# A growing lead for the scores at the start of a two-problem attention kernel, with TensorE transposes of the remainder's P in the ramp and round the change of weights

## The chip, the core and the metric

The kernel runs on one core of a Trainium2 chip. Times are device microseconds (us). The kernel before was run three times: 1224.69, 1225.98 and 1227.50 us, median 1225.98 us. One execution was taken by the hardware profiler; its own time is 1227.16 us.

Engines are called as in the profile: PE is TensorE's matmul, PEld its weight load, DVE VectorE, ACT ScalarE, POOL GpSimd, and SP the engine whose queue issues all DMAs here.

## What is computed

Two independent attention blocks A and B of the same shape, bfloat16, whose outputs stand side by side:

```python
B, Sq, D = 16, 144, 448;  H, Sk, Dh = 16, 512, 256
q = (x @ wq).reshape(B, Sq, H, Dh).transpose(0, 2, 1, 3)
scores = einsum("bhqd,bhkd->bhqk", q, k_cache) * Dh ** -0.5
p = softmax(scores)                                  # over the 512 keys
o = einsum("bhqk,bhkd->bhqd", p, v_cache)
out = o.transpose(0, 2, 1, 3).reshape(B, Sq, H * Dh) @ wo
# result: concatenate([out_A, out_B], axis=-1)
```

## The kernel before, in words

**Units and groups.** A unit U is one head of one batch element; there are 2 x 256 = 512 of them (0 to 255 are A, 256 to 511 B). The 144 queries of a unit are split: 112 rows ("a") have a score matmul of their own, and the remaining 32 rows ("b", the remainder) of four units are packed together to 128 rows, a quad G. Eight units (two quads) form a group SG; there are 64 groups. A group's K (2 MB) comes by one DMA that transposes it, and V comes by quads (1 MB each).

**What one unit does**, with the names and lines of the profile:

- Q: eight matmuls into the PSUM bank `qp_ps` (L322), copied to `qt_sb` by DVE (L334) or ACT (L338).
- SA: the scores of the 112 rows, two matmuls into one of two banks `sa_ps` (L424). Then max on DVE (L435), exp with its row sum on ACT (L446), the reciprocal on DVE (L456), and on POOL the multiplication of P by it (L464).
- SB, once a group: the remainder's scores of eight units, 16 matmuls into the two banks `sb_ps` (L348), with max, exp (L371), reciprocal (L381) and multiplication (L389) for each quad.
- TA: P of the 112 rows is transposed by four PE instructions into a bank of `sa_ps` (L477), copied to `pt_sb` by DVE (L487).
- The remainder's P is transposed for a whole group by one DMA from `pb_sb` to the single buffer `pbt_sb` (L399), and POOL copies it, a quad at a time, to its place in `pt_sb` (L410, `t_copy_ptb`).
- PV: eight matmuls of V and P into `ot_ps` (L510), copied by ACT into `ring` (L525).
- OP: the output projection over finished rows of 128 (L548), two matmuls at a time, at 2.5 matmuls a slot from slot 34 on; the result is copied and stored.

**Order.** A planner written in Python walks over slots i. Each engine's instructions run in the order in which this walk emits them; a scheduler adds the semaphore waits that the buffers need. Slot i has PV of unit i, TA of unit i+2, SA of unit i+14, Q of unit i+22, and SB of a group when its first SA is due. So the walk starts with 22 slots with Q and without PV; slot 0 is the first with PV. "Lead of the scores" is the distance between SA and PV: 14 units.

**DMAs** are in a list of (slot, order), walked by the same loop, so SP issues them in one fixed order and a waiting one holds those behind it: x0, weights wq 0 and 1, K0, wq 2 and 3, K1, the remainder's P of group 0, V0 to V2, x1, K2, and so on. There are two buffers for K, five for V, two for x. K of group n+2 may be issued once the last SA of group n has run. From the second group on, each pair of groups n, n+1 (n even) has the transposes of P at slots 8n-4 and 8n+2, K at 8n-3 and 8n+2, four V at 8n+5 to 8n+8, and x every 32 units. wo is loaded by eight parts for each problem, at slots 21 and 37 (and 256 later for B). The wq of B replaces that of A by four parts, at slots 229, 229, 232 and 235, behind three V of slot 229:

```python
plan((5, 5, 8, 11)[hg] + NU - 32, lo, dl, t_load_wq, 1, hg)
```

Q(256), the first that needs them, stands in slot 234.

Of the kernel before, what the change touches and what calls it, by code (L numbers as in the profile page):

```python
# [5 lines left out]
BF16 = mybir.dt.bfloat16  # L6
# [116 lines left out]
def bass_concat_heads__mha_block_cached__gqa_block_cached__near_ridge_kernel(  # L123
# [19 lines left out]
    Bn, SQ, D = A_x.shape  # L143
# [4 lines left out]
    NU = Bn * H  # L148
    NT = NP * NU
    NG = NT // 4  # L150
    HG = H // 4
    NCH = (Bn * SQ + 127) // 128
    RP = NCH * 128
# [4 lines left out]
    NWG = NWO // WOG  # L158
    NPC = NWO // OPP

    LQ, LS, LT = 22, 14, 2
    LSB = 14
    NK, NV, NXG = 2, 5, 2
    WO_AT = ((21, 37), (21, 37))
    OP_FROM = (34, 34)
    XB = 2
    assert Bn % XB == 0
    NQT, NPA, NPB, NPT, NST, NSTB, NOST = 12, 14, 2, 8, 4, 2, 3
    NPBT = 1
# [1 line left out]
    RC = RS * 128  # L171
    OP_DELAY = 2
    assert NT % 8 == 0
    NSG = NT // 8
    NXGT = NP * Bn // XB

    of = out.rearrange("b q e -> (b q) e")

    with contextlib.ExitStack() as es:
# [23 lines left out]
        ot_ps = [ps("ot_ps%d" % i, [128, 512], F32) for i in range(2)]  # L203
        op_ps = ps("op_ps", [128, 512], F32)
        pta_ps = [t.bitcast(BF16) for t in sa_ps]

        S = _Sched()
        sem_names = list(COMPUTE)
# [25 lines left out]
        def t_ident():  # L234
            ones = pa_sb[:, 0, 0:128]

            def e1(g):
                return g.memset(ones, 1.0)
            S.add(POOL, e1, writes=[(("pa", 0), "ones")], name="ones")

            def e2(g):
                return g.affine_select(ident[:], ones, pattern=[[1, 128]], compare_op=ALU.is_equal,
                                       fill=0.0, base=0, channel_multiplier=-1)
            S.add(POOL, e2, reads=[(("pa", 0), "ones")], writes=[("ident", 0)], name="ident")

        def t_wqzero():
            def e(v):
# [53 lines left out]
        def t_load_v(G):  # L301
# [5 lines left out]
                return q.dma_start(v_sb[:, sl, :, :], src).then_inc(sems["v%d" % sl], 16)  # L307
            S.add(SP, e, writes=[(("v", sl), G)], dma_sem="v%d" % sl, name="v%d" % G)

        def t_q(U):  # L310
            pr, b, h = unit(U)
            XG = (pr * Bn + b) // XB
            xsl = XG % NXG
            xo = (b % XB) * SQ
            hg = h // 4

            def e(t):
                ins = None
                for kc in range(4):
                    for dc in range(2):  # L320
                        c0 = h * DH + dc * 128
                        ins = t.matmul(qp_ps[:, dc * SQ:(dc + 1) * SQ], lhsT=wq_sb[:, kc, c0:c0 + 128],  # L322
                                       rhs=xt_sb[:, xsl, kc, xo:xo + SQ], start=(kc == 0 and dc == 0),
                                       stop=(kc == 3), skip_group_check=True)
                return ins
            S.add(PE, e, reads=[(("wq", hg), pr), ("wqz", 0), (("xt", xsl), XG)], writes=[("qp", ("q", U))],
                  banks=["qp"], name="Q%d" % U)

        def t_evac_q(U):
            sl = U % NQT  # L330
            src = qp_ps[:, 0:2 * SQ].rearrange("p (c q) -> p c q", c=2)
            if (U - LQ + LSB) % 8 in (1, 3, 5, 6):
                def e(v):
                    return v.tensor_scalar(qt_sb[:, sl, :, :], src, 1.0 / 16.0, None, op0=ALU.mult)  # L334
                S.add(DVE, e, reads=[("qp", ("q", U))], writes=[(("qt", sl), U)], banks=["qp"], name="eq%d" % U)
            else:
                def e(a):
                    return a.activation(qt_sb[:, sl, :, :], src, AF.Copy, scale=1.0 / 16.0)  # L338
                S.add(ACT, e, reads=[("qp", ("q", U))], writes=[(("qt", sl), U)], banks=["qp"], name="eq%d" % U)

        def t_sb(SG):
            def e(t):
# [51 lines left out]
        def t_ptb_dma(SG):  # L394
            psl = SG % NPB
            tsl = SG % NPBT

            def e(q):
                return q.dma_start_transpose(pbt_sb[:, tsl, :, :, :].rearrange("p g c q -> p (g c) q"),  # L399
                                             pb_sb[:, psl, :, :].rearrange("p g k -> p (g k)")).then_inc(  # L400
                    sems["pb%d" % tsl], 16)
            S.add(SP, e, reads=[(("pb", psl, g), (2 * SG + g, 1)) for g in range(2)], writes=[(("pbt", tsl), SG)],
                  dma_sem="pb%d" % tsl, name="pb%d" % SG)

        def t_copy_ptb(G):
            tsl = (G // 2) % NPBT
            s0 = (4 * G) % NPT

            def e(g):
                return g.tensor_copy(pt_sb[:, s0:s0 + 4, :, QA:SQ],  # L410
                                     pbt_sb[:, tsl, G % 2, :, :].rearrange("p c (j q) -> p j c q", j=4))
            S.add(POOL, e, reads=[(("pbt", tsl), G // 2)], writes=[(("ptb", s0 + j), 4 * G + j) for j in range(4)],
                  name="cptb%d" % G)

        def t_sa(U):
# [52 lines left out]

        def t_ta(U):
            psl = U % NPA  # L470
            bank = (U + LS - LT + 1) % 2

            def e(t):
                src = pa_sb[0:QA, psl, :].rearrange("q (p c) -> q c p", c=4)
                ins = None
                for c in range(4):
                    ins = t.transpose(pta_ps[bank][:, c * 128:c * 128 + QA], src[:, c, :], ident[0:QA, 0:QA])  # L477
                return ins
            S.add(PE, e, reads=[(("pa", psl), (U, 1)), ("ident", 0)], writes=[(("sap", bank), ("t", U))],
                  banks=["sa%d" % bank], name="TA%d" % U)  # L480

        def t_evac_pta(U):
            sl = U % NPT
            bank = (U + LS - LT + 1) % 2

            def e(v):
                return v.tensor_copy(pt_sb[:, sl, :, 0:QA],  # L487
# [94 lines left out]
        t_act_warm()  # L582
        t_wqzero()
        t_ident()
        s_min = -LQ - 24
        dma_plan = []

        def plan(at, lo, dl, fn, *args):
            assert lo <= at < dl, (fn.__name__, args, lo, at, dl)
            dma_plan.append((at, len(dma_plan), fn, args))  # L590

        def plan_k(at, SG):
            plan(at, 8 * (SG - NK) + 7 - LS + 1 if SG >= NK else s_min, 8 * SG - LSB, t_load_k, SG)

        def plan_v(at, G):
            plan(at, 4 * (G - NV) + 3 + 1 if G >= NV else s_min, 4 * G, t_load_v, G)

        def plan_pb(at, SG):
            plan(at, 8 * SG - LSB + 5, 8 * SG - 1, t_ptb_dma, SG)

        plan(s_min, s_min, -LQ, t_load_x, 0)
        for hg in range(HG):
            plan(s_min + (1 if hg < 2 else 3), s_min, 4 * hg - LQ, t_load_wq, 0, hg)
        plan_k(s_min + 2, 0)
        plan_k(s_min + 4, 1)
        for G in range(3):
            plan_v(-7, G)
        for pr in range(NP):
            for wg in range(NWG):
                plan(pr * NU + WO_AT[pr][wg // 4], s_min, pr * NU + OP_FROM[pr] + wg, t_load_wo, pr, wg)  # L610
        for n in range(0, NSG, 2):
            t = 8 * n
            XG = (t + 32) // (XB * H)
            if (t + 32) % (XB * H) == 0 and XG < NXGT:
                plan(t - 4, (XG - 1) * XB * H - LQ, XG * XB * H - LQ, t_load_x, XG)
            plan_pb(t - 4 if n else -8, n)
            if n + 2 < NSG:
                plan_k(t - 3, n + 2)
            plan_pb(t + 2, n + 1)
# [3 lines left out]
                if 2 * n + 3 + j < NG:  # L623
                    plan_v(t + at, 2 * n + 3 + j)
        for hg in range(HG):
            dl = NU + 4 * hg - LQ
            lo = NU - H + 4 * hg + 3 - LQ + 1
            plan((5, 5, 8, 11)[hg] + NU - 32, lo, dl, t_load_wq, 1, hg)
        dma_plan.sort(key=lambda t: t[:2])

        u_tail0 = NT - H
# [32 lines left out]
        while True:  # L664
            while dma_plan and dma_plan[0][0] <= i:
                _sl, _sq, fn, args = dma_plan.pop(0)
                fn(*args)
            sgi, ph = divmod(i + LSB, 8)
            do_sb = ph == 0 and 0 <= sgi < NSG
            ga, gb = 2 * sgi, 2 * sgi + 1  # L670
            ok = 0 <= sgi < NSG
            if ok and ph == 1:
                t_exp_b(ga)
            if ok and ph == 3:
                t_exp_b(gb)
            if ok and ph == 2:
                t_recip_b(ga)
                t_norm_b(ga)
            if ok and ph == 4:
                t_recip_b(gb)  # L680
                t_norm_b(gb)
            while stores and stores[0][1] <= i and (i % 16 in (9, 10, 11) or i >= NT - 4):
                t_store(stores.pop(0)[0])
            if do_sb and sgi == 0:
                t_sb(sgi)
            u = i + LQ
            if 0 <= u < NT:
                t_q(u)
                t_evac_q(u)
            if do_sb and sgi > 0:  # L690
                t_sb(sgi)
            u = i + LS
            if 0 <= u < NT:
                t_sa(u)
                t_max(u)
                t_exp(u)
            if i % 8 == 7 and 0 <= i + 1 < NT:
                t_copy_ptb((i + 1) // 4)
            if i % 8 == 1 and 0 <= i < NT:
                t_copy_ptb((i + 3) // 4)  # L700
            u = i + LS - 1
            if 0 <= u < NT:
                t_recip(u)
                t_norm(u)
            u = i + LT
            if 0 <= u < NT:
                t_ta(u)
                t_evac_pta(u)
            if ok and ph == 0:
                t_max_b(ga)  # L710
            if ok and ph == 2:
                t_max_b(gb)
            u = i
            if 0 <= u < NT:
# [92 lines left out]
```

## Time and profile before

| | us |
|---|---|
| median of three runs | 1225.98 |
| the profiled execution | 1227.16 |
| its span in the profile | 1225.4 |
| PE busy | 1167.7 (95%) |
| PEld busy | 877.0 (72%) |
| ACT busy | 745.6 (61%) |
| DVE busy | 730.3 (60%) |
| POOL busy | 728.6 (59%) |

The DMA engines move 310.87 MB at a mean of 254 GB/s. A digit in the page's rows of forty slices is the busy share of 30.6 us in tenths; PEclk is TensorE's granted clock in tenths of full speed. Matmuls are pipelined, so the start of one to the start of the next says more than the duration of one. In a row of the timeline the bracket is the engine's idle time just before it and what ended it.

### The profile page before, as it was taken

Reading aid. Unit: us, or ns where it says so; the run is one execution under the profiler, and the core shown is the slowest. Engines: PE = TensorE matmul, PEld = TensorE weight load, DVE = VectorE, ACT = ScalarE, POOL = GpSimd, SP = SyncE. Lnnn points to the kernel's source line nnn. Section 1 sums busy time; section 2 is a strip of 40 time slices with the busy share of each in tenths; the row PEclk is TensorE's granted clock in tenths of the full one; section 3 lists DMA queues with packets and bytes.
Section 4 is the critical chain, followed back from the end, with each engine's and each line's share of the span. In section 5 each row is a group of like instructions: output and inputs, shape, how many; then the busy total and the mean of one; then the engine's idle time right before and its main releaser. Section 6 shows DMA issues by size and latency. Waiting matters only on the chain.

```text
span 1225.4 us, 32870 instructions
## 1 busy us (share of the span) xinstructions
PE 1167.7 (95%) x13440; PEld 877.0 (72%) x13440; DVE 730.3 (60%) x2051; ACT 745.6 (61%) x2213; POOL 728.6 (59%) x774
## 2 busy tenths in 40 slices
PE   5698899999999999999899989999999999999999
PEld 3476667777777777777567757777777777777766
DVE  2577456666666566666456646666666666666661
ACT  2476466666666566666556656666666666666662
POOL 0676556666666666666456646656666665666661
PEclk9899899999999999999899989999999999999999
DMA  9999999999999999999999999999999999999982
GB/s 219 266 271 280 286 275 216 259 263 271 269 229 237 268 277 257 272 242 257 289 282 256 227 290 283 273 266 265 218 262 265 264 256 277 255 225 260 257 209 55
DMA packets 698583, 310.87 MB, mean 254 GB/s; under 512 B 616512, under 2 KB 629312, under 8 KB 698432
## 3 DMA queue, kind: packets, MB, share of 16 engines
q1 hardware_dynamic: 698432, 308.77, 106.3%
q8 instruction: 105, 1.72, 0.6%
q14 instruction: 46, 0.38, 0.1%
HBM read 148.90 MB, written 4.13 MB: 125 GB/s over the span
## 4 chain that ended last, share of the span: by engine, by line
PE 78%; DMA 15%; DVE 3%; POOL 2%; issue 2%; SPq 0%; ACT 0%; DVEq 0%
PE qp_ps L322 17%; PE ot_ps L510 17%; PE sa_ps L424 16%; PE op_ps L548 16%; DMA kt_sb<-in_A_k_cache_dram 8%; PE sa_ps L477 7%; PE sb_ps L348 6%; DMA kt_sb<-in_B_k_cache_dram 5%; POOL pa_sb L464 1%; DVE stat L435 1%; DMA v_sb<-in_A_v_cache_dram 1%; DVE qt_sb L334 1%; PE qp_ps L548 0%; DVE pt_sb L487 0%; DMA pbt_sb<-pb_sb 0%
## 5 line engine op out<-in xcount | busy, mean ns | idle before, releaser
L464 POOL TENSOR_TENSOR pa_sb<-pa_sb,stat 112x512 bf16<-112x512 bf16 x512 | 532.8, 1041 | 458.7 <-DVE stat L456 430.5
L446 ACT ACTIVATE pa_sb<-sa_ps,stat 112x512 bf16<-112x512 f32 x512 | 351.9, 687 | 408.1 <-DVE stat L435 405.7
L435 DVE TENSOR_REDUCE stat<-sa_ps 112x1 f32<-112x512 f32 x512 | 354.0, 691 | 366.2 <-PE sa_ps L424 361.7
L322 PE MATMUL qp_ps<-xt_sb,wq_sb 128*128 128x144 bf16 x4096 | 346.5, 229 | 22.2 <-DMA wq_sb<-in_A_wq_dram 9.4
L322 PEld LDWEIGHTS qp_ps<-xt_sb,wq_sb 128*128 128x128 bf16 x4096 | 290.7, 99 | 100.9 <-issue 15.5
L510 PE MATMUL ot_ps<-pt_sb,v_sb 128*128 128x144 bf16 x4096 | 343.1, 227 | 9.0 <-POOL pt_sb L410 8.3
L424 PE MATMUL sa_ps<-kt_sb,qt_sb 128*112 128x512 bf16 x1024 | 315.8, 390 | 4.7 <-DVE pt_sb L487 3.5
L510 PEld LDWEIGHTS ot_ps<-pt_sb,v_sb 128*128 128x128 bf16 x4096 | 270.2, 98 | 9.7 <-POOL pt_sb L410 8.6
L548 PE MATMUL op_ps<-wo_sb,ring 128*128 128x448 bf16 x1120 | 275.5, 353 | 0.0
L477 PEld LDWEIGHTS sa_ps<-ident,pa_sb 112*128 112x128 bf16 x2048 | 159.9, 114 | 109.2 <-ACT pa_sb L446 32.2
L525 ACT ACTIVATE ring<-ot_ps 128x288 bf16<-128x288 f32 (+8 forms) x512 | 189.9, 371 | 27.1 <-PE ot_ps L510 27.0
L487 DVE COPY pt_sb<-sa_ps 128x448 bf16<-128x448 bf16 x512 | 191.1, 373 | 17.7 <-PE sa_ps L477 17.7
L477 PE MATMUL sa_ps<-ident,pa_sb 112*128 112x112 bf16 x2048 | 187.6, 214 | 0.4 <-ACT pa_sb L446 0.4
L334 DVE TENSOR_SCALAR qt_sb<-qp_ps 128x288 bf16<-128x288 f32 x256 | 117.0, 457 | 103.1 <-PE qp_ps L322 102.6
L389 POOL TENSOR_TENSOR pb_sb<-pb_sb,stat 128x512 bf16<-128x512 bf16 x128 | 133.3, 1041 | 0.0
L424 PEld LDWEIGHTS sa_ps<-kt_sb,qt_sb 128*112 128x112 bf16 x1024 | 96.9, 130 | 47.3 <-issue 28.8
L338 ACT ACTIVATE qt_sb<-qp_ps 128x288 bf16<-128x288 f32 x256 | 105.9, 414 | 40.3 <-PE qp_ps L322 40.0
L548 PEld LDWEIGHTS op_ps<-wo_sb,ring 128*128 128x128 bf16 x1120 | 96.2, 98 | 32.0 <-issue 0.4
L446 ACT ACTIVATION_READ_ACCUMULATOR pa_sb<-sa_ps,stat 112x1 f32 x512 | 98.9, 193 | 0.0
L410 POOL COPY pt_sb<-pbt_sb 128x512 bf16<-128x512 bf16 x128 | 78.2, 611 | 21.3 <-PE ot_ps L510 10.9
L348 PE MATMUL sb_ps<-kt_sb,qt_sb 128*32 128x512 bf16 x1024 | 72.1, 405 | 18.6 <-DMA kt_sb<-in_A_k_cache_dram 12.3
L371 ACT ACTIVATE pb_sb<-sb_ps,stat 128x512 bf16<-128x512 f32 x128 | 88.3, 690 | 0.0
(20 smaller groups left out, 306.3 us busy)
## 6 DMA issues: line engine op xcount, KB each, us to landing
v_sb<-in_A_v_cache_dram SPq DMA_DIRECT2D x64, 1024.0 KB, 9.4
v_sb<-in_B_v_cache_dram SPq DMA_DIRECT2D x64, 1024.0 KB, 9.4
out_dram<-ost_sb SPq DMA_DIRECT2D x36, 112.0 KB, 10.2
wo_sb<-in_A_wo_dram SPq DMA_DIRECT2D x8, 448.0 KB, 5.0
wo_sb<-in_B_wo_dram SPq DMA_DIRECT2D x8, 448.0 KB, 5.7
wq_sb<-in_A_wq_dram SPq DMA_DIRECT2D x4, 768.0 KB, 6.6
wq_sb<-in_B_wq_dram SPq DMA_DIRECT2D x4, 768.0 KB, 13.1
pbt_sb<-pb_sb SPq DMA_TRANSPOSE x64, 4.6
```

Of the source, the lines that this page charges most:

```text
L322: ins = t.matmul(qp_ps[:, dc * SQ:(dc + 1) * SQ], lhsT=wq_sb[:, kc, c0:c0 + 128], rhs=xt_sb[:, xsl, kc, xo:xo + SQ], start=(kc == 0 and dc ...
L348: ins = t.matmul(sb_ps[jj // 4][32 * j:32 * j + 32, :], lhsT=qt_sb[:, U % NQT, dc, QA:SQ], rhs=kt_sb[:, dc, (U % (8 * NK)) * SK:(U % (8 * ...
L389: return g.tensor_tensor(pb_sb[:, psl, G % 2, :], pb_sb[:, psl, G % 2, :], stat[:, RINVB + sl:RINVB + sl + 1].to_broadcast([128, SK]), op= ...
L424: ins = t.matmul(sa_ps[bank][0:QA, :], lhsT=qt_sb[:, U % NQT, dc, 0:QA], rhs=kt_sb[:, dc, ko:ko + SK], start=(dc == 0), stop=(dc == 1))
L435: return v.tensor_reduce(stat[0:QA, NEG + sl:NEG + sl + 1], sa_ps[bank][0:QA, :], axis=AX.X, op=ALU.max, negate=True)
L446: return a.activation(pa_sb[0:QA, psl, :], sa_ps[bank][0:QA, :], AF.Exp, bias=stat[0:QA, NEG + sl:NEG + sl + 1], scale=1.0, accum_out=stat ...
L464: return g.tensor_tensor(pa_sb[0:QA, psl, :], pa_sb[0:QA, psl, :], stat[0:QA, RINV + sl:RINV + sl + 1].to_broadcast([QA, SK]), op=ALU.mult)
L477: ins = t.transpose(pta_ps[bank][:, c * 128:c * 128 + QA], src[:, c, :], ident[0:QA, 0:QA])
L487: return v.tensor_copy(pt_sb[:, sl, :, 0:QA], pta_ps[bank][:, 0:512].rearrange("p (c q) -> p c q", c=4)[:, :, 0:QA])
L510: ins = t.matmul(ot_ps[ob][:, dc * SQ:(dc + 1) * SQ], lhsT=v_sb[:, vsl, j, c * DH + dc * 128:c * DH + (dc + 1) * 128], rhs=pt_sb[:, sl, c, ...
L525: ins = a.activation(ring[:, 2 * h:2 * h + 2, c0:c0 + n1], src[:, :, 0:n1], AF.Copy)
L548: ins = t.matmul(acc[0:m, 0:D], lhsT=ring[:, c, col0:col0 + m], rhs=wo_sb[:, c, :], start=(c == first), stop=(c == last))
```

## The change

The lead is no longer fixed. `LAGS` gives the distance between the start of group n's scores (SB, then its SA) and its first PV: 7 for group 0, then 5, 6, 7 and so on to 14 for group 10 and all later ones. So groups 1 to 10 start at slots 3, 10, 17, 24, 31, 38, 45, 52, 59 and 66, seven slots apart, and the first slot of each of groups 1 to 9 has two SA. From slot 82 on the order is that of before. Q runs eight units ahead of SA, as before; the first eight Q come together one slot before the first SA, over four PSUM banks (`q_bank`), with 12 matmuls on zeros before them and 16 behind them (`t_warm`).

For groups 0 to 7 and 28 to 37 (`TB_SG`) the remainder's P is transposed by PE (`t_tb`, four instructions a quad, into a bank of `sb_ps`) and copied by DVE (`t_evac_tb`), and its DMA is left out. In the ramp the two TB stand three and five slots behind SB, but not before slot 8n-7; for groups 28 to 37 both stand in slot 8n-7, one slot before the next group's SB. Bank choice of TA (`ta_bank`): the bank that the slot's last SA doesn't use.

The DMA order of the ramp is written anew: x0, wq 0 and 1, K0, wq 2 and 3, V0, K1, V1, V2, K2, V3, V4, x1, K3, and so on, K and then two V a group. wo of A comes by pairs at slots 12, 18, 26 and 33. wq 0 and 1 of B stand at 228.9, ahead of the V of slot 229.

```diff
-    LQ, LS, LT = 22, 14, 2
-    LSB = 14
+    LT = 2
+    LAGS = (7, 5, 6, 7, 8, 9, 10, 11, 12, 13, 14)
+    RAMP = 8
+    TB_SG = set(range(RAMP)) | set(range(NSG // 2 - 4, NSG // 2 + 6))
-    WO_AT = ((21, 37), (21, 37))
+    WO_AT = ((12, 18, 26, 33), (277, 277, 293, 293))
+    N_WARM = (12, 16)
...
+        ptb_ps = [t.bitcast(BF16) for t in sb_ps]
...
+        def t_warm_zero():
+            def e(v):
+                return v.memset(pa_sb[:, 2:6, 0:128], 0.0)
+            S.add(DVE, e, writes=[("warm", 0)], name="warmz")
...
+        def q_bank(U):
+            if U >= 8:
+                return qp_ps, "qp", "qp"
+            return ((qp_ps, "qp", "qp"), (op_ps, "opp", "op"), (ot_ps[0], ("otp", 0), "ot0"),
+                    (ot_ps[1], ("otp", 1), "ot1"))[U % 4]
...
-            if (U - LQ + LSB) % 8 in (1, 3, 5, 6):
+            if U % 8 in (1, 3, 5, 6):
...
+        def t_warm(k):
+            def e(t):
+                ins = None
+                for _ in range(N_WARM[k]):
+                    ins = t.matmul(sb_ps[1][:, :], lhsT=ident[:, :], rhs=pa_sb[:, 2:6, 0:128], start=True, stop=True)
+                return ins
+            S.add(PE, e, reads=[("ident", 0), ("warm", 0)], writes=[(("sbb", 1), ("w", k))], banks=["sb1"],
+                  name="W%d" % k)
...
+        def t_tb(G):
+            psl = (G // 2) % NPB
+
+            def e(t):
+                ins = None
+                for c in range(4):
+                    ins = t.transpose(ptb_ps[G % 2][:, c * 128:(c + 1) * 128],
+                                      pb_sb[:, psl, G % 2, c * 128:(c + 1) * 128], ident[:, :])
+                return ins
+            S.add(PE, e, reads=[(("pb", psl, G % 2), (G, 1)), ("ident", 0)], writes=[(("sbb", G % 2), ("t", G))],
+                  banks=["sb%d" % (G % 2)], name="TB%d" % G)
+
+        def t_evac_tb(G):
+            tsl = (G // 2) % NPBT
+
+            def e(v):
+                return v.tensor_copy(pbt_sb[:, tsl, G % 2, :, :],
+                                     ptb_ps[G % 2][:, 0:512].rearrange("p (c q) -> p c q", c=4))
+            S.add(DVE, e, reads=[(("sbb", G % 2), ("t", G))], writes=[(("pbt", tsl, G % 2), G // 2)],
+                  banks=["sb%d" % (G % 2)], name="etb%d" % G)
...
-            bank = (U + LS - LT + 1) % 2
+            bank = ta_bank[U]
...
+        lag = [LAGS[min(n, len(LAGS) - 1)] for n in range(NSG)]
+        sb_slot = [8 * n - lag[n] for n in range(NSG)] + [8 * NSG - lag[-1]]
+        sa_slot = [sb_slot[u // 8] + (u % 8) * (sb_slot[u // 8 + 1] - sb_slot[u // 8]) // 8 for u in range(NT)]
+        q_slot = [sb_slot[0] - 1] * 8 + sa_slot[:NT - 8]
...
+        for n in TB_SG:
+            t0 = 8 * n - 7
+            tb_at.setdefault(max(sb_slot[n] + 3, t0), []).append(2 * n)
+            tb_at.setdefault(max(sb_slot[n] + 5, t0), []).append(2 * n + 1)
...
         def plan_pb(at, SG):
-            plan(at, 8 * SG - LSB + 5, 8 * SG - 1, t_ptb_dma, SG)
+            if SG not in TB_SG:
+                plan(at, sb_slot[SG] + 5, 8 * SG - 1, t_ptb_dma, SG)
...
+        plan_x(s_min, 0)
         for hg in range(HG):
-            plan(s_min + (1 if hg < 2 else 3), s_min, 4 * hg - LQ, t_load_wq, 0, hg)
+            plan(s_min + (0 if hg < 2 else 1), s_min, q_slot[4 * hg], t_load_wq, 0, hg)
+            if hg == 1:
+                plan_k(s_min, 0)
+        plan_v(s_min + 2, 0)
+        for n in range(1, RAMP + 2):
+            at = max(sb_slot[n] - 6, sa_slot[8 * (n - NK) + 7] + 1) if n >= NK else s_min + 2
+            if n == 3:
+                plan_x(at, 1)
+            if n == 6:
+                plan_x(at, 2)
+            plan_k(at, n)
+            plan_v(at + 1, 2 * n - 1)
+            plan_v(at + 1, 2 * n)
...
-            plan((5, 5, 8, 11)[hg] + NU - 32, lo, dl, t_load_wq, 1, hg)
+            plan((4.9, 4.9, 8, 11)[hg] + NU - 32, lo, q_slot[NU + 4 * hg], t_load_wq, 1, hg)
...
+            if i == q_slot[0]:
+                t_warm(0)
+                for u in range(8):
+                    t_q(u)
+                    t_evac_q(u)
+                t_warm(1)
+            sas = sa_at.get(i, ())
+            for u in sas:
+                if 8 <= u and u + 8 < NT:
+                    t_q(u + 8)
+                    t_evac_q(u + 8)
+                if u % 8 == 0:
+                    t_sb(u // 8)
                 t_sa(u)
+                if u < 8:
+                    t_q(u + 8)
+                    t_evac_q(u + 8)
                 t_max(u)
                 t_exp(u)
+                last_sa = u
...
             if 0 <= u < NT:
+                ta_bank[u] = 1 - last_sa % 2 if sas else u % 2
                 t_ta(u)
                 t_evac_pta(u)
-            if ok and ph == 0:
+            for G in tb_at.get(i, ()):
+                t_tb(G)
+                t_evac_tb(G)
+            if ph == 0:
                 t_max_b(ga)
```

## The prediction

> **What bounds the kernel now.** I read the page first (busy shares, the forty slices), then the waits, the timeline of PE, the timeline of SP's queue, and the DMA rate in one early stretch.
>
> ```profile
> span 1225.4 us, 32870 instructions
> ...
> PE   5698899999999999999899989999999999999999
> ...
> PEclk9899899999999999999899989999999999999999
> DMA  9999999999999999999999999999999999999982
> ```
>
> PE works nine tenths of nearly every slice. The holes are in slices 1 to 7 (30.6 us each: the ramp) and round slices 20 and 24 (the change of weights), and there the clock digit drops too. The DMA row is full everywhere, also where PE has holes.
>
> ```profile
> PE qp_ps L322 <- DMA wq_sb<-in_A_wq_dram: 9.4, 1, 9.4
> PE ot_ps L510 <- POOL pt_sb L410: 8.3, 2, 5.5
> PE sb_ps L348 <- DMA kt_sb<-in_A_k_cache_dram: 12.3, 7, 5.8
> PE sb_ps L348 <- DMA kt_sb<-in_B_k_cache_dram: 5.6, 4, 2.8
> PE qp_ps L322 <- issue: 4.9, 1, 4.9
> ```
>
> These are PE's own waits (total, times, longest). Of its 57.7 us idle (1225.4 less 1167.7 busy), K transfers take 18, the remainder's P (PV behind the POOL copy L410) 8.3, and the "issue" row is Q(256) at 591.6, when the first new weights landed (591.5). The PE timeline places them: 5.75 at 57.8, 5.47 at 125.4, 1.52 at 131.9, 2.46 at 171.3, 4.87 at 591.6, 2.77 at 615.2, 2.83 at 721.3, 2.20 at 727.5. Elsewhere slots run back to back:
>
> ```profile
> 265.65 0.66 PE L322 MATMUL qp_ps<-xt_sb,wq_sb 128*128 128x144 bf16 x8
> ...
> 266.15 0.59 PE L424 MATMUL sa_ps<-kt_sb,qt_sb 128*112 128x512 bf16 x2
> ...
> 266.58 0.36 PE L477 MATMUL sa_ps<-ident,pa_sb 112*128 112x112 bf16 x4
> ...
> 266.78 0.67 PE L510 MATMUL ot_ps<-pt_sb,v_sb 128*128 128x144 bf16 x8
> ...
> 267.28 0.92 PE L548 MATMUL op_ps<-wo_sb,ring 128*128 128x448 bf16 x4
> ```
>
> Start to next start gives PE's prices at full clock: Q 0.50, SA 0.43, TA 0.20, PV 0.50; by the same reading SB 0.98 per group of 8 and one OP matmul 0.19. At 2.5 OP matmuls a slot that is 2.23 us; groups are 18.05 apart, 2.26 a slot.
>
> ```profile
> 109.35 7.04 SPq L287 DMA_TRANSPOSE xt_sb<-in_A_x_dram  x1
> 116.43 1.26 SPq L288 DMA_TRANSPOSE xt_sb<-in_A_x_dram  x1
> 117.74 2.85 SPq L399 DMA_TRANSPOSE pbt_sb<-pb_sb  x1
> 120.63 9.20 SPq L297 DMA_TRANSPOSE kt_sb<-in_A_k_cache_dram  x1
> ```
>
> This is SP just before the 5.47 and 1.52 holes: x held it 7 us, so the transpose of P that PV needed, and the K behind it, came late.
>
> ```profile
> GB/s 78 290 290 290 290 290 290 283 223 24 262 396 251 404 358 404 390 407 391 401 389 272 248 13 33 227 289 285 146 291 293 34 283 290 289 291 273 157 169 129
> ```
>
> That is the DMA answer for 30 to 60 us (0.75 us each): K moves at 290 GB/s, V at 400, with dips at each change between kinds. Landing to landing, behind other work: V 2.7 us; one wo part 1.2; x 2.6 to 3.2; the transpose of P 0.7 behind others and about 2.0 alone; K, over thirteen cases, 7.0 to 10.2, mean 8.75. So without OP a group of eight needs 8.75 + 5.4 + about 2 = 16.2 us of DMA and 14.0 of PE: **the early stretch is bound by DMA, the rest by PE.**
>
> **Part 1, the start.** Before, Q 0 to 7 ran on one bank at half clock (1.14 us each instead of 0.66) with 0.5 gaps, and SB0 started at 22.78. Now four banks and W0 (12 matmuls, from about 3.3 us, at 0.43 cold at most 5.2, so done before the weights land at 9.36): Q 0 to 3 take 9.45 to 11.5, Q 4 to 7 wait for their weights (landed 13.03) and end at 15; W1's 16 x 0.22 = 3.5 fills to 18.6; SB0 goes when K0 lands, 20.13. Then Q8 waits for weights that land at 23.64. V0 is now ahead of K1, so K1 lands at 36.3 + 2.7 = 39.0. Until then PE has SB0, 8 SA, 8 Q, 5 TA, 3 PV, 2 TB, about 12 us bare from 23.64, at the softmax pace that 28 to 45 us shows (1.4 us a unit) near 38. SB1 is at 39.2, in slot 3 instead of slot -6. K1 sets it, so what the warm-up saves is mostly swallowed.
>
> **Part 2, to slot 38, by DMA.** V1, V2: 44.5. K2: 53.2. V, V, x1, K3: 5.6 + 2.7 + 8.75, 70.2. V, V, two wo, K4: 5.6 + 2.45 + 8.75, 87.0. Again, K5: 103.8. Again with x2 (2.8), K6: 123.4. PE for 7 slots wants 8 x (0.50 + 0.43 + 0.12) + 7 x 0.70 + two TB 0.46 + small gaps 0.3 + the wait described next 0.8 = 14.9, less than each 16.8 of DMA with wo, so the 8 TB added up to here cost nothing; without that cover, 0.46 a group. SB6 stands at 123.4 in slot 38; before, slot 38 came at 131.9 + 4 x 2.35 = 141.3. (The earlier kernel has scored four units more by then, which Part 3 makes up.) In this sum five DMA transposes of P have left SP and the DMA engines (0.7 to 2.0 each), and all of wo instead of half is loaded (+4.9).
>
> A new wait: in a slot with two SA, TA takes the bank of the first, whose exp ends 1.7 us after it (max 0.69, exp 0.69, accumulator 0.19), while PE has 0.93 of Q and SA between: 0.8 a group. PV, OP and the next Q queue behind it on PE.
>
> **Part 3, slots 38 to 82, by PE.** 8.4 + 7 x (0.20 + 0.50 + 0.47) + 0.3 + 0.8 = 17.7 for seven slots, 18.1 with TB; K needs 14.2. Two with TB and 1.0 of half clock after the last K wait, two without, two of 8 slots at 18.05: 123.4 + 37.2 + 35.4 + 36.1 = 232.1 for SB12. Before, with the same work done, 245.0: **12.9 us gained**. If K moves at its 7.2 (2.1 MB at 290 GB/s) PE itself holds SB6 to about 118 and it is 18; with K at 9.8, five K make it 8.
>
> **Part 4, the change of weights.** New weights 0 and 1 go ahead of three V (8.1 us): they land at about 585, before Q(256) wants them (586.7), and the 4.87 disappears. But K32 lies behind the same four weight parts and four V (580.41 to 604.50 before, 24.1 us). K31 starts 1.6 earlier, since no transpose of P stands before it on SP, so K32 lands at 578.8 + 24.1 + 8.75 = 611.6 instead of 615.1. PE wants it at 586.7 + 8 x 2.26 = 604.8. **The wait moves to SB32 and 3.5 us are gained, not 4.87 + 2.77.** The displaced V (used from slot 236, 591 us) land by 588 to 593: in time. SB38 is alike: the 2.83 goes (no transpose of P to wait for), K38 saves the 2.4 that SP spent on it and lands at about 725 less 0 to 1.5, against 727.5: total 3. Ten groups pay TB 0.46 plus about 0.1 of waiting for DVE's two extra copies ahead of SB: the cptb that the second copy needs ends 1.05 us before SB, the copy is 0.43. Half of that lies under the K waits; SB38 holds the rest except 0.5 behind. Gain 2.5, between 0 and 6.
>
> **Sum.** 1227.2 (profiled: span 1225.4 and 1.8 round it) - 12.9 - 2.5 = 1211.8; the median of the runs stands 1.2 below the profiled one: 1210.6.
>
> The price of TB rests on TA's row: 4 transposes of 112 columns in 0.20, so 0.23 with 128. The Trainium skill, "TensorE: Matmul & The Clock Gate", Part 4, speaks against the change: a transpose of 128 by 128 is put at about 275 ns within a kernel, 1.1 us for a TB. By that each of some 18 TB that nothing covers would cost 0.87 more, an estimate of 15 us, and the result would be about 1226. The row is the same operation in this kernel, so I take the row. That page's table of goals also says that only gaps over about 3 us slow the clock; here the 2.20 gap is followed by an SB of 1.90 instead of 1.05, so I charge shorter gaps too.
>
> **Rivals.**
> - *DMA yields more.* Without transposes between, K runs at 290 GB/s without dips: 7.2 each, then SB6 comes at 116 to 118, when PE is ready; the middle gives 6. About 1200. For it: dips at changes of kind. Against: thirteen landings. 0.13.
> - *Warm-up without effect.* From 9.45 to 27 us PE stayed slow at 70% busy. Then Q 4 to 7 end at 18.6, W1 takes 16 x 0.43 = 6.9, SB0 starts at 25.5, later than before. SB2 slips to 59; DMA still rules from K4 on: 1212. 0.10.
> - *Slower: TB at the head of PE's queue.* A TB needs POOL's normalised P. That ends 6.45 and 10.15 us after SB (before, slots of 1.8 us); PE reaches the two TB at about 7.0 and 10.7 (Q of the third and fifth slot after SB at 5.9 and 9.6, and 1.1 of Q, SA and TA). The margin is 0.5. If POOL or DVE lag (early on DVE is wanted 8 x 1.07 for max, reciprocal and half of Q's copies, 7 x 0.37 for P's copies, 2 x 1.25 for the remainder: 13.7 of 14.9 us a group), PE and all behind it stand. It decides from 15.4 / 36 = 0.43 us a TB, beyond what DMA hides; at 0.75 each, 1227 - 15 + 27 = 1239, less 1.2: 1238. 0.10. Against: double slots move TB later by 0.9.
>
> **How the numbers follow.** The forecast has 0.67, by itself 1204 to 1217 (K at 7.2 or 9.8 in Part 3, Part 4 from 0 to 6, not all at once). The range reaches halfway into the first rival and above the forecast to what a shallow form of the slower one leaves: 1200 to 1222. 0.2% is 2.5 us, about what a measurement can tell from no change. Faster takes the forecast and two rivals but a little: 0.88; the slower rival leaves 0.09 slower; 0.03 within.
>
> **What would show it.** SB1 at 38 to 41; SB6 near 123, waiting for K there and at SB4 and SB5; SB12 near 232; no wait at Q(256) but one of about 6 us on K at SB32; no wait of PV on L410's POOL copy; TB at 0.22 to 0.25. Wrong if PE waits on TB's source, if SB2 or SB3 waits for the softmax, or if groups 6 to 9 stand over 18.5 apart.

## The result and the profile after

The changed kernel takes 1215.51 us (median of four, 1215.11 to 1215.99), the kernel before, on the same chip, 1226.24 us; the ratio is 0.9913 with a 95% interval of 0.9896 to 0.993. That is 10.7 us less, where 15.4 had been forecast (1210.6 against 1226.0); it lies in the range of 1200 to 1222. The profiled execution took 1215.54 us, its span is 1213.8.

These are the page's rows for the changed kernel, the same ones as shown of before:

```profile
span 1213.8 us, 33200 instructions
...
PE   6898999999999999999899989999999999999989
...
PEclk9998999999999999999899999999999999999999
DMA  9999999999999999999999999999999999999982
```

The holes of the ramp are smaller, those round slices 20 and 24 remain in part, and the DMA row is as full as before. PE's own waits (total, times, longest):

```profile
PE sb_ps L374 <- DMA kt_sb<-in_B_k_cache_dram: 11.3, 5, 5.3
PE sb_ps L374 <- DMA kt_sb<-in_A_k_cache_dram: 6.5, 4, 3.2
PE sa_ps L524 <- ACT pa_sb L493: 6.1, 9, 0.7
...
PE qp_ps L338 <- DMA wq_sb<-in_A_wq_dram: 4.2, 3, 1.8
...
PE sb_ps L437 <- POOL pb_sb L415: 1.0, 1, 1.0
```

Gone are the waits of PV on the POOL copy (8.3) and of Q(256) (4.9). The wait for the first weights reads 4.2 instead of 9.4 only because the matmuls on zeros fill it: the first Q starts at 9.47, before at 9.45. K of A costs half of its 12.3. But K of B costs twice its 5.6: that is where the wait at the change of weights went. New are nine waits of TA on ACT, 0.7 each: the first TA, at 30.9, and eight of the nine slots with two SA. In the order of the kernel, from PE's timeline:

```profile
19.98 1.05 PE L374 MATMUL sb_ps<-kt_sb,qt_sb 128*32 128x512 bf16 x16 [1.45 <-DMA kt_sb<-in_A_k_cache_dram]
...
107.85 1.90 PE L374 MATMUL sb_ps<-kt_sb,qt_sb 128*32 128x512 bf16 x16 [3.20 <-DMA kt_sb<-in_A_k_cache_dram]
...
601.26 1.90 PE L374 MATMUL sb_ps<-kt_sb,qt_sb 128*32 128x512 bf16 x16 [5.28 <-DMA kt_sb<-in_B_k_cache_dram]
...
713.84 1.54 PE L374 MATMUL sb_ps<-kt_sb,qt_sb 128*32 128x512 bf16 x16 [3.38 <-DMA kt_sb<-in_B_k_cache_dram]
```

These are SB0, SB5, SB32 and SB38. The rows of 1.90 instead of 1.05 show half clock after the wait: the granted clock from 107.85 to 111.26 is 0.50. With the start of SB as the mark of each group:

| | before | forecast | after |
|---|---|---|---|
| SB0 | 22.8 | 20.1 | 20.0 |
| SB1 | 37.9 (slot -6) | 39.2 (slot 3) | 40.9 |
| SB4 | 91.1 (slot 18) | 87.0 (slot 24) | 88.9 |
| SB6 | 131.9 (slot 34) | 123.4 (slot 38) | 127.8 |
| SB12 (slot 82) | 245.0 | 232.1 | 235.5 |
| ahead at SB12 | | 12.9 | 9.5 |
| ahead at SB27 | | | 10.4 |
| ahead at SB32 | | 3.5 more by K32 | 13.9 |
| ahead at SB38 | | | 13.7 |
| ahead at the end of the span | | 15.4 | 11.6 |

SB12, on which much of what follows rests, reads before and after:

```profile
245.00 1.05 PE L348 MATMUL sb_ps<-kt_sb,qt_sb 128*32 128x512 bf16 x16
```
```profile
235.49 1.05 PE L374 MATMUL sb_ps<-kt_sb,qt_sb 128*32 128x512 bf16 x16
```

So the profile splits the gain into 9.5 in the ramp, 3.3 round the change of weights, about 1 in between and about 2 lost again late. A second profile of the changed kernel, given at the end of the experiments, has 10.5 in the ramp, 0.5 in between and 1.8 round the change of weights: marks and their differences are good to 1 to 1.5 us, and the middle gain is known no better than that.

### The profile page after: what moved, and what is told of

Same layout as the page of the kernel before. It is cut to its first block, busy times and chain, and to the rows that moved or that the text cites. A ratio compares the mean times of both kernels' runs of the same rounds, so it can differ in the third digit from the quotient of the medians.

```text
span 1213.8 us, 33200 instructions
## 1 busy us (share of the span) xinstructions
PE 1171.0 (96%) x13612; PEld 882.9 (73%) x13612; DVE 743.7 (61%) x2088; ACT 748.6 (62%) x2213; POOL 727.9 (60%) x774
## 3 DMA queue, kind: packets, MB, share of 16 engines
q8 instruction: 107, 1.75, 0.6%
## 4 chain that ended last, share of the span: by engine, by line
PE 80%; DMA 12%; DVE 3%; POOL 2%; SPq 1%; issue 1%; ACT 1%; DVEq 0%
PE ot_ps L557 17%; PE qp_ps L338 17%; PE sa_ps L471 16%; PE op_ps L595 16%; PE sa_ps L524 7%; DMA kt_sb<-in_A_k_cache_dram 6%; DMA kt_sb<-in_B_k_cache_dram 6%; PE sb_ps L374 5%; POOL pa_sb L511 1%; DVE stat L482 1%; SPq L306 1%; POOL pb_sb L415 1%; PE sb_ps L437 1%; ACT pa_sb L493 1%; PE qp_ps L595 1%
## 5 line engine op out<-in xcount | busy, mean ns | idle before, releaser
L338 PEld LDWEIGHTS qp_ps<-xt_sb,wq_sb 128*128 128x128 bf16 x4048 | 284.1, 98 | 81.6 <-DMA wq_sb<-in_A_wq_dram 3.9
L338 PE MATMUL qp_ps<-xt_sb,wq_sb 128*128 128x144 bf16 x4048 | 337.4, 227 | 4.6 <-DMA wq_sb<-in_A_wq_dram 4.2
L387 DVE TENSOR_REDUCE stat<-sb_ps 128x1 f32<-128x512 f32 x128 | 87.2, 681 | 0.0
L374 PE MATMUL sb_ps<-kt_sb,qt_sb 128*32 128x512 bf16 x1024 | 69.2, 391 | 18.2 <-DMA kt_sb<-in_B_k_cache_dram 11.3
```

Of the source, the lines that this page charges most:

```text
L338: ins = t.matmul(acc[:, dc * SQ:(dc + 1) * SQ], lhsT=wq_sb[:, kc, c0:c0 + 128], rhs=xt_sb[:, xsl, kc, xo:xo + SQ], start=(kc == 0 and dc = ...
L374: ins = t.matmul(sb_ps[jj // 4][32 * j:32 * j + 32, :], lhsT=qt_sb[:, U % NQT, dc, QA:SQ], rhs=kt_sb[:, dc, (U % (8 * NK)) * SK:(U % (8 * ...
```

## The experiments

The experiments ran on three chips, each beside the kernel before. Runs of one variant scatter by 3 to 12 us there (the kernel before from 1221 to 1231), so each variant is read by its marks in the profile and by the median together; where a ratio is given, it is to the kernel before on the same chip.

### Which part of the early change brings the 9.5

**No warm-up matmuls.**

```diff
-                t_warm(0)
-                t_warm(1)
```

> The changed kernel without its 28 warm-up matmuls. My theory: SB0 goes when K0 lands (19.85 in the changed kernel), and eight Q over four banks end by about 17.5 even at half clock (1.0 each from 9.45), so SB0 stays at 20; later groups 4 and 5 wait for K anyway. Median 1215.5, between 1215 and 1217. Rival, the start's gain comes from the warm clock: SB0 at 22 or later and 3 to 5 us more, about 1219.

Measured: 1217.19 us. PE's timeline of this run:

```profile
8.98 1.12 PE L338 MATMUL qp_ps<-xt_sb,wq_sb 128*128 128x144 bf16 x8 [8.98 <-DMA wq_sb<-in_A_wq_dram]
...
13.42 0.66 PE L338 MATMUL qp_ps<-xt_sb,wq_sb 128*128 128x144 bf16 x8 [0.63 <-DMA wq_sb<-in_A_wq_dram]
...
20.56 1.90 PE L374 MATMUL sb_ps<-kt_sb,qt_sb 128*32 128x512 bf16 x16 [4.98 <-DMA kt_sb<-in_A_k_cache_dram]
```

The first Q are slow (1.12), but back to back over four banks they reach full speed after 4 us by themselves, and SB0 still goes when K0 lands (20.42). SB0 then runs at half clock, but that isn't what is left at the end of the ramp: SB5 comes at 106.8 and SB6 at 127.7, no later than with the warm-up (107.9 and 127.8). SB12 is at 236.6, 1.1 later, behind a wait of 2.72 for K6. The median lies just above my range, and the rival's 3 to 5 are not there. By the medians the warm-up is worth about 2 us, by SB12 1.1 (2.1 against the second profile), which is the size of the scatter.

**The old fixed lead, all else as changed.**

```diff
-    LAGS = (7, 5, 6, 7, 8, 9, 10, 11, 12, 13, 14)
+    LAGS = (14,)
```

> The changed kernel with the old fixed lead of 14 units (LAGS of one entry), all else as changed: order of the first DMAs, TB in the ramp and in the middle, wo by pairs, warm-up. My theory: the stretch up to SB6 is set by the DMA chain, which is the same bytes in nearly the same order, so SB6 comes at about 126 to 127 again, only four slots earlier in the order (34 instead of 38). Four slots of TA, PV and OP are 4 x 1.17 = 4.7 us behind, and four waits of TA in slots with two SA, 0.67 each, are saved: 2 us worse, 1217.5 (1216 to 1219.5). Rival, the growing lead brings the early gain of 9.5: about 1224.

Measured: 1216.54 us (ratio 0.9935, 0.9915 to 0.9956), SB6 at 125.5, SB12 at 235.5, the same as with the growing lead. **The growing lead, which gives the change its name, is worth nothing that can be measured.** K5 is waited for in both (3.62 here). With the growing lead SB6 is 2.3 later, with four more slots of TA, PV and OP done (4.7 by the expectation's estimate); the waits of TA in the four double slots from there on take 2.7 of that back, so that both are level at SB12. The slots of wo did not move with the lead, so its place among K and V is another one here. SB1 stands at 37.4 against 37.9 in the kernel before: of the earlier start little is left by then.

**The same, and the remainder's P of the first eight groups by DMA again.**

```diff
-    LAGS = (7, 5, 6, 7, 8, 9, 10, 11, 12, 13, 14)
+    LAGS = (14,)
-    TB_SG = set(range(RAMP)) | set(range(NSG // 2 - 4, NSG // 2 + 6))
+    TB_SG = set(range(NSG // 2 - 4, NSG // 2 + 6))
+        for n in range(RAMP):
+            plan_pb(-8 if n == 0 else 8 * n - (6 if n % 2 else 4), n)
```

> As the kernel with the fixed lead of 14, and the remainder's P of the first eight groups by DMA again (at the places of the kernel before); the new order of the first DMAs, wo by pairs, the warm-up and the middle stay. It splits the early gain of 9.5, which the lead of 14 kept whole (SB12 at 235.5 in both). My theory now: TB brings it, because eight transposes of P leave the DMA chain (0.7 to 2.0 each) and no K stands behind one that waits for POOL: SB12 at 241 to 244, median about 1223. Rival, the order brings it (V, wo and x where K doesn't wait for them): SB12 at 236 to 238, median about 1218.

Measured: 1229.57 us, slower than the kernel before (ratio 1.0025, 1.0009 to 1.0041), and above both my 1223 and the rival's 1218; SB6 at 135.8 and SB12 at 244.9, where the kernel before has 245.0. First SB12 with the fixed lead and TB, then SB12 of this kernel and its waits:

```profile
235.47 1.05 PE L374 MATMUL sb_ps<-kt_sb,qt_sb 128*32 128x512 bf16 x16
```
```profile
244.85 1.05 PE L374 MATMUL sb_ps<-kt_sb,qt_sb 128*32 128x512 bf16 x16
```

```profile
PE sb_ps L374 <- DMA kt_sb<-in_A_k_cache_dram: 14.7, 7, 4.0
...
PE ot_ps L557 <- POOL pt_sb L457: 8.6, 2, 6.8
```

Without TB the whole early gain is gone, and the wait of PV is back. The new order of DMAs and the new start alone bring nothing there. This kernel has both middle edits, and from SB27 to SB38 it takes 210.95, as the kernel before (210.96): the gain of the middle, too, is not there without the early one.

**TB alone in the kernel before.**

```diff
         def plan_pb(at, SG):
-            plan(at, 8 * SG - LSB + 5, 8 * SG - 1, t_ptb_dma, SG)
+            if SG >= 8:
+                plan(at, 8 * SG - LSB + 5, 8 * SG - 1, t_ptb_dma, SG)
...
+            if i >= -7 and (i + 7) % 8 == 0 and (i + 7) // 8 < 8:
+                for G in (2 * ((i + 7) // 8), 2 * ((i + 7) // 8) + 1):
+                    t_tb(G)
+                    t_evac_tb(G)
```

> The kernel before with one thing alone added: the remainder's P of the first eight groups by TB (both in slot 8n-7), their DMA transposes left out. Old lead of 14, old order of DMAs, no warm-up, nothing in the middle. My theory: this alone is the early gain; SB12 at 236 to 238 instead of 245.0, and the median about 8 below the kernel before: 1218 (1216 to 1220). Rival, TB only pays with the new order of the first DMAs or the new start: SB12 at 241 or later, 1222 or more.

Measured: 1224.24 us (ratio 0.9993, 0.9975 to 1.0012: no difference), SB12 at 241.0. My 236 to 238 was wrong and the rival right: TB needs the new order.

```profile
57.05 1.90 PE L349 MATMUL sb_ps<-kt_sb,qt_sb 128*32 128x512 bf16 x16 [4.86 <-DMA kt_sb<-in_A_k_cache_dram]
...
240.99 1.05 PE L349 MATMUL sb_ps<-kt_sb,qt_sb 128*32 128x512 bf16 x16 [1.32 <-DMA kt_sb<-in_A_k_cache_dram]
```

These are SB2 and SB12. SB2 of the kernel with the lead of 14, TB and the new order:

```profile
53.40 1.05 PE L374 MATMUL sb_ps<-kt_sb,qt_sb 128*32 128x512 bf16 x16 [1.42 <-DMA kt_sb<-in_A_k_cache_dram]
```

Part of what the order brings stands here. In the old order x lies ahead of K2: its issue starts at 42.7 instead of 36.3, it lands at 56.9 instead of 53.3, SB2 waits longer, and the granted clock from 57 to 73 us is 0.81 instead of 1.00. At SB3 the two kernels are 5.5 apart. The wait for K5 (3.62, in the new order only) leaves 2.1 of that at SB5. What brings it back to 5.5 by SB12 is seen in the queue and the DMA rate. First the old order with TB, SP's timeline and the stretch from 73 to 92 us (busy us of the engines, granted clock, DMA share, GB/s):

```profile
64.02 7.48 SPq L308 DMA_DIRECT2D v_sb<-in_A_v_cache_dram x4
73.99 25.52 SPq L298 DMA_TRANSPOSE kt_sb<-in_A_k_cache_dram  x2
```
```profile
73.00:92.00 19.00, 18.55 (x241) 14.02 (x242) 13.83 (x40) 13.60 (x40) 13.90 (x15) 1.00 0.85 202
```

And the new order:

```profile
67.78 14.08 SPq L306 DMA_TRANSPOSE kt_sb<-in_A_k_cache_dram  x1
...
83.08 1.06 SPq L316 DMA_DIRECT2D v_sb<-in_A_v_cache_dram  x2
84.18 2.38 SPq L285 DMA_DIRECT2D wo_sb<-in_A_wo_dram  x2
86.60 16.32 SPq L306 DMA_TRANSPOSE kt_sb<-in_A_k_cache_dram  x1
```
```profile
73.00:92.00 19.00, 18.63 (x234) 13.96 (x234) 14.03 (x41) 13.84 (x41) 13.28 (x15) 1.00 1.14 307
```

In the old order four V go together and two K then follow each other; the second K waits for its buffer (its issue starts at 90.2, K4 having landed at 87.9), and the DMA engines have nothing else: 202 GB/s, and none at all from about 86 to 91 us. In the new order K, V and wo alternate in the queue: 307 GB/s. The dry stretch costs nothing at once, as PE is busy in 18.55 of these 19 us. Behind it SB6 waits 4.00 for K6 instead of 1.21, and SB12 waits 1.32 for K12; that these waits pay for the dry stretch is argued from the order of the queue, no run isolates it. **The early gain is TB and the order together:** the order (with the new start) alone 0, TB alone 4.0, both 9.5, measured at SB12. Which part of the order brings how much (V0 ahead of K1, x behind K2, wo by pairs) wasn't separated, nor were the four banks of the first Q.

### The change of weights

**P of groups 28 to 37 by DMA again.**

```diff
-    TB_SG = set(range(RAMP)) | set(range(NSG // 2 - 4, NSG // 2 + 6))
+    TB_SG = set(range(RAMP))
```

> The changed kernel with the remainder's P of groups 28 to 37 transposed by DMA again (TB in the ramp alone). My theory: transposes of P stand on SP before K31, K32 and K38 again, so SB32 comes 2 to 3 us later than the changed kernel's 601.3, PV of unit 288 waits again for the POOL copy, SB38 comes 2 to 3 us later, and the 0.45 of TB a group is saved only where no K wait swallows it: 1217.5 (1216 to 1219). Rival, TB on a busy PE costs more there than it brings (0.45 a group was lost from group 31 to 37): 1213.

Measured: 1217.24 us; SB32 at 604.6 and SB38 at 716.6, 3.4 and 2.8 later than in the changed kernel (2.5 and 1.9 later than in its second profile). PE's timeline:

```profile
598.32 1.14 PE L557 MATMUL ot_ps<-pt_sb,v_sb 128*128 128x144 bf16 x8 [6.06 <-POOL pt_sb L457]
```

Here the transpose of P stands behind the new weights and PV waits 6.06 for it; K32, behind that, is late as well. As expected, but for the place: the larger of the two waits of PV stands ahead of SB32, and the one ahead of SB38 is 1.94.

**Weights 0 and 1 of B behind the three V again** (two sets of runs).

```diff
-            plan((4.9, 4.9, 8, 11)[hg] + NU - 32, lo, q_slot[NU + 4 * hg], t_load_wq, 1, hg)
+            plan((5, 5, 8, 11)[hg] + NU - 32, lo, q_slot[NU + 4 * hg], t_load_wq, 1, hg)
```

> The changed kernel with the weights 0 and 1 of B behind the three V again. My theory: Q(256) waits again 3 to 5 us, but SB32 is set by K32, which lies behind the same weights and V, so SB32 stays near 601 and only some half clock is added: 1216 (1215 to 1217.5). Rival, the order of the weights brings the gain in the middle: 4 us more, 1219.5.

> The kernel with weights 0 and 1 of B behind the three V once more, for a profile of its commoner time (its runs fell at 1209.7 and at 1218 to 1219.5). My theory: the middle gains no more than 2 us over the changed kernel and the rest is K waits that come and go between executions: 1211 to 1217. Rival, the old order of the weights is really better by 5 us: 1209 to 1211 again, and the profile shows SB39 over 4 us ahead of the changed kernel's 734.2 with SB27 level.

Measured: 1211.40 us (ratio 0.9905, 0.9876 to 0.9935) and 1213.58 us (0.9897, 0.9876 to 0.9918), against 0.9913 and 0.9922 for the changed kernel: not slower, as my 1216 and the rival's 1219.5 had it at first, but, if anything, 1 to 4 us faster. (Three executions of the first set took 1209.7; what made them so quick stays open. Its one profile, of an execution of 1219.47, is already 3.9 late at SB27, so what made that one slow lies ahead of the weights.) In the profile of the second set:

```profile
580.88 1.12 PE L338 MATMUL qp_ps<-xt_sb,wq_sb 128*128 128x144 bf16 x8 [3.75 <-issue]
...
602.40 1.05 PE L374 MATMUL sb_ps<-kt_sb,qt_sb 128*32 128x512 bf16 x16 [0.29 <-DMA kt_sb<-in_B_k_cache_dram]
```

Q(256) waits 3.75 again, and SB32 then has only 0.29 to wait instead of 5.28. SB39 stands at 733.2 against 734.2, with SB27 at 505.6 against 506.2. K32 lands at 602.3 here, at 601.1 and 601.9 in the changed kernel's two profiles: it sets the size of the stall, and the order of the weights only chooses where PE stands still. The rival's claim that the old order is really better by 5 us isn't borne out by the marks.

**Both middle edits undone.**

> The changed kernel with both middle edits undone: the remainder's P of groups 28 to 37 by DMA, and weights 0 and 1 of B behind the three V. The start and the ramp stay as changed. In the kernel before plus TB alone, the 4 to 5 us that stood ahead at SB27 were gone at SB38: PE came earlier to weights and K that the DMA chain sets. My theory: this chain starts from K30 and K31, which PE releases, so it moves with PE; what is ahead at SB27 (10) is kept but for 1 to 2, and the order of the weights adds nothing to the 1217.2 of the kernel with the middle by DMA: 1217.5 (1216 to 1219.5), Q(256) waiting 5 and SB32 2 to 5. Rival, the chain is bound by bytes from further back and swallows the early gain as it did there: SB38 at 721 or later, 1221 to 1225.

Measured: 1218.24 us (ratio 0.9932, 0.9908 to 0.9957). Ahead of before by 8.7 at SB27 and 8.8 at SB38: the early gain is kept. That it vanished at this place in the kernel before with TB alone (5.0 ahead at SB27, level at SB38, Q(256) waiting 7.06 there) is therefore no rule; why there and not here stays open. By the medians TB in the middle is worth 2 us with the new order of the weights (1217.2 against 1215.5) and 5 to 7 with the old (1218.2 against 1211.4 and 1213.6). The marks from SB27 to SB39 say the same, 1.0 to 2.6 and 4.2 to 5.6; the intervals of the ratios overlap in both cases.

### Moving what the stalls wait for

**K32 ahead of weights 3 and V of quad 62.**

```diff
-                    plan_v(t + at, 2 * n + 3 + j)
+                    plan_v(238 if 2 * n + 3 + j == 62 else t + at, 2 * n + 3 + j)
...
-            plan((4.9, 4.9, 8, 11)[hg] + NU - 32, lo, q_slot[NU + 4 * hg], t_load_wq, 1, hg)
+            plan((4.9, 4.9, 8, 13.5)[hg] + NU - 32, lo, q_slot[NU + 4 * hg], t_load_wq, 1, hg)
```

> The changed kernel, with weights 3 of B and V of quad 62 issued behind K32 instead of ahead of it (Q(268) and PV(248), which need them, stand four and six slots after SB32). My theory: K32 is the bound of SB32 by what lies ahead of it, so it lands 5 us earlier, SB32 stands at 595.5 to 597 instead of 601.3 without the wait of 5.28 and with no half clock after it: 1209 (1207.5 to 1211.5). Rival, the stall only moves to K33 or K38, which the same DMA chain sets: 1214 to 1215.5.

Measured: 1214.90 us. PE's timeline shows SB32 and SB34:

```profile
596.91 1.05 PE L374 MATMUL sb_ps<-kt_sb,qt_sb 128*32 128x512 bf16 x16 [0.98 <-DMA kt_sb<-in_B_k_cache_dram]
```
```profile
636.84 1.16 PE L374 MATMUL sb_ps<-kt_sb,qt_sb 128*32 128x512 bf16 x16 [3.68 <-DMA kt_sb<-in_B_k_cache_dram]
```

SB32 came 4.4 earlier, and K34, behind what had been put back, took 3.68 of it; at SB39 1.1 is left. Most of the stall only moved, as the rival had it (though to K34, not to K33 or K38), and my 1209 was wrong.

**All of these moves: the one before, x behind K from group 8 on, two parts of wo of B behind K38, wo and x2 behind K6.**

```diff
-    WO_AT = ((12, 18, 26, 33), (277, 277, 293, 293))
+    WO_AT = ((12, 18, 32.5, 36), (277, 285.5, 293, 293))
-                plan_x(at, 2)
+                plan_x(at + 0.25, 2)
-                plan_x(t - 4, XG)
+                plan_x(t - 2.5, XG)
```

> The edit of the one before; every x from group 8 on issued behind the K that it stood ahead of; two parts of wo of B behind K38; and in the ramp two pairs of wo and x2 behind K6. My theory: K38's wait of 3.38 goes (4 us of wo and x leave its way), the K waits of groups 18, 46 and 54, which stand behind an x, go too (0.6 to 0.9 each), and SB5 and SB6 come 2 to 4 us earlier: 1203 (1200 to 1207). Rival, the ramp and steady state are bound by PE and by the sum of bytes: as the one before, 1208 to 1211.

Measured: 1208.06 us (ratio 0.9846, 0.9825 to 0.9867), just above my range and at the lower end of the rival's. SB5 and SB6 did not move by much (108.3, 126.4), so that part of my reason fell; SB38 came 6.4 earlier than in the changed kernel (707.4) and no longer waits for K; SB34 and SB40 now wait 2.7 and 2.1 for K. Behind that one K wait over 0.6 is left, 1.32.

**The same with the fixed lead.** The moves of the kernel just above, with `LAGS = (14,)`:

> The kernel with all moves of DMAs (K32, K38 and K6 first, x behind K), and the fixed lead of 14. My theory: the lead brings nothing, so it equals the one with the growing lead: 1208 (1205 to 1211), SB12 at 234.5 to 236.5. Rival, with K6 freed of wo and x2 the stretch from SB6 on is bound by PE, where the short lead has four units of PV done more: 3 to 5 us slower, 1212.

Measured: 1207.08 us (ratio 0.9851, 0.9826 to 0.9876), SB12 at 234.0. No difference between the two medians, and the rival's 1212 is out: the lead brings nothing here either. Both are faster than the kernel before and the changed kernel; the fixed lead is the simpler.

**The changed kernel once more.**

> The changed kernel again, unchanged, beside the others on one chip and for a second profile. If the K waits at groups 46, 54 and 60 (2.7 in all, against 0.65 in the same stretch of the kernel before) belong to the program they come again; my theory is that they come and go with the DMA engines' timing and that the whole stays at 1214 to 1217.

Measured: 1214.74 us, with SB12 at 234.5, SB32 at 602.1, SB38 at 714.7. The late K waits came again at the same groups 46, 54 and 60 (1.46, 0.60 and 0.56), 2.6 in all against 2.7: their sizes vary, their sum didn't. My theory that they come and go isn't borne out by these two profiles. Yet the profile of the changed kernel with the fixed lead, whose order is the same at these groups, has 0.2 there in all, so what makes them stays open.

## Why the prediction was right, and which terms were mis-sized

**The mechanism held.** The ramp was bound by DMA and then by PE; PE waited for K at SB4 (1.01) and SB5 (3.20); nothing waits at Q(256), and SB32 waits 5.28 where "about 6" was forecast. The gain from SB27 to SB32 is 3.5, the very figure; to SB38 it is 3.3 where 2.5 was forecast. That the first agrees so well is luck: the second profile has 2.1 and 1.8. Its parts differ too. Counted from SB27, K31 landed 2.8 and 2.9 earlier than before, not 1.6; the weights and V behind it took 24.8 and 26.4 instead of 24.1, and K32 9.0 instead of 8.75. From SB33 to SB36 the lead over the kernel before shrinks by 0.45 a group, which is the price of two TB. All three rivals fell: K did not come at 7.2; the first Q took 0.67, so the warm-up had its effect on the clock; and TB waited for POOL in few places (the 1.0 above, at 32.3, and 2.4 in six weight loads): the sign of being wrong that the prediction named for it showed once, and small.

**The term of the DMA in Part 2 was too small.** From K3 to K6 the chain took 57.1 us (landings at 69.67, 88.79, 107.71, 126.79) and not 53.2. V were not 2.7 each there: behind K3 and behind K4 two took 7.8 and 7.0 us. K itself took 9.0, 8.7 and 10.3. What slows V there isn't shown (see the last section).

**The half clock stood in another place.** I charged 1.0 after the last K wait. The stretch from SB5 to SB6 reads (last columns: granted clock, DMA share, GB/s):

```profile
107.85:127.85 20.00, 19.82 (x206) 14.29 (x210) 11.85 (x33) 10.31 (x30) 10.41 (x11) 0.86 1.18 270
```

A granted clock of 0.86 over 20 us is 2.8 lost (0.91 and 1.8 in the second profile), and it made PE, not K6 (landed at 126.79), the bound at SB6: it starts without a K wait at 127.8. K6 came 3.4 late and SB6 another 1.0; the 1.0 returned behind it, since Part 3 had charged it there, and 3.4 are missing at SB12. The rest of Part 3 agrees: SB7 to SB10 follow 18.2, 18.2, 17.1 and 18.1 after the group ahead, where 18.1, 18.1, 17.7 and 17.7 were forecast; the wait of TA is 0.67 against 0.8. SB1 came at 40.9 instead of 39.2, set by the softmax (four waits of 0.7 to 1.3) and not, as forecast, by K1 (37.3); later K waits swallowed that.

**Late waits on K took 2.0 that the sum did not have:** 0.59, 0.91 and 1.17 at groups 46, 54 and 60, where the kernel before has 0.65 in all after SB39. The second profile has 2.6 at the same three groups, so they aren't one execution's; but with the fixed lead there are 0.2, and what makes them stays open.

**What the prediction did not separate.** It summed the lead, TB and the order in one DMA chain. The runs show that the chain was the right object, and that the lead in it counts for nothing. The misses (3.4 in the ramp, 2.0 late) are made up in part by about 1 between SB12 and SB27 and 0.8 in the middle that weren't forecast, so the total of 10.7 against 15.4 looks a little better than its terms.

The rule weighed against the row: TB from its own row takes 0.23 (124.08 to the PV at 124.31 in PE's timeline of the changed kernel), as TA's row had let expect:

```profile
124.08 0.39 PE L437 MATMUL sb_ps<-ident,pb_sb 128*128 128x128 bf16 x4
124.31 0.66 PE L557 MATMUL ot_ps<-pt_sb,v_sb 128*128 128x144 bf16 x8
```

By the 275 ns for one transpose within a kernel that the Trainium skill gives ("TensorE: Matmul & The Clock Gate", Part 4) a TB would be 1.1 us, an estimate; the measurement decides for 0.06 each in a stream. The record of one such transpose lasts 0.22 us here too (median of 144), but four of them overlap and take 0.23 from start to next start.

## What to carry to other kernels

Where a stage is bound by the DMA queue, ask which transfers stand in it, what lies ahead of the one that is waited for, and whether the queue ever runs dry. Here, taking a small transfer out that waits for another engine and holds the queue, together with another order of the rest, brought the early gain; the lead of the scores did nothing. A stall in front of such a chain wasn't removed by reordering its first member; ask which transfer ends the chain, and what that one waits for. Split a change into its parts by experiment before crediting the part it is named after.

## What the runs showed of the hardware

- Some short waits cost more than themselves: after 3.20 us without matmuls, SB took 1.90 instead of 1.05, and the mean granted clock of the next 20 us was 0.86. After a wait of 1.01 (SB4) SB took its 1.05. After the two waits of 1.45 and 1.75 near 20 and 23 us, Q at 26.1 took 1.17 instead of 0.66, and the granted clock from 22.7 to 27 us was 0.74.
- Without the warm-up, Q back to back from 8.98 reached full speed by 13.4 (1.12, then 0.66); in the kernel before, with a gap of 0.5 after each, Q were still slow at 21 us (1.14). The granted clock in the profile reads 1.00 in both stretches, from 9 to 13 us and from 9.4 to 22.7: so early only the durations tell.
- In the changed kernel four V between 69 and 99 us took 3.3 to 4.3 us from landing to landing instead of 2.7, while a transposing K was being issued behind them. Three others, with K's issue running too, landed after 2.6 to 2.7 (at 133.1, 147.7 and 150.3), so the issue alone doesn't explain it.
